# Sooner query loads and unturned inner gradients in a four-layer forward and backward kernel on one Trainium2 core

## The chip, the cores and the metric

The kernel runs on one core of a Trainium2 chip (trn2). The metric is the device time of one execution in microseconds (us). Three timed executions of the kernel before the change took 1105.07, 1106.90 and 1107.01 us; the median is 1106.9 us. One more execution was recorded by the profiler; it took 1113.49 us, and its recorded span is 1111.6 us.

The names used below: PE is the matrix engine (PEld its weight loads), DVE the vector engine, ACT the scalar engine, POOL the GpSimd engine, SP the sync engine, which here only issues DMAs. DMAs are issued from two engines: from SP (all loads, all transposing DMAs, most stores) and from POOL (the stores written as `k.st.dma_start`). Each engine works through its own list in order, so an instruction that waits holds up everything behind it on that engine.

## What is computed

The forward pass has four layers on x of 2048 tokens by 512: linear attention (l=0), a gated unit or GLU (l=1), linear attention with the same weights (l=2), the GLU again (l=3). Each is `x = x + layer(layernorm(x))`.

```python
def A(x):   # 32 heads of 16
    q, k, v = split(x @ wqkv)
    pq, pk = phi(q), phi(k)          # phi(t) = where(t > 0, t + 1, exp(t)) + 1e-6
    kv, z = sum_s(pk * v), sum_s(pk)
    return ((pq @ kv) / (pq . z + 1e-6)) @ wo
def B(x):   # inner width 1376
    return (sigmoid(x @ w_gate) * (x @ w_up)) @ w_down
```

The outputs are the result, and the gradients of x, wqkv, wo, w_gate, w_up and w_down for a given gradient of the result, all in bfloat16.

## The kernel before

**Tiling.** Tokens are cut into 16 tiles of 128 rows, four tiles to a block (`NBLK` = 4 blocks of 512 tokens, `SB` = 512). The inner width 1376 is cut into 11 chunks (`NFC`) of 128; as 1376 is 10 times 128 plus 96, the last chunk starts at 1248 and repeats 32 rows (`FDUP`) of the tenth (`FC0`). A matmul here takes a 128x128 weight block and 512 columns.

**Stages, in order of time.**
1. l=0 forward (`AFwd.first`, `AFwd.second`), to about 74 us, its second half running on into l=1.
2. l=1 forward (`b_fwd`, L671), 74 to 214 us: for each block, 11 chunks of gate and up products (`glu`, L642), then the down product of the block before (`down`, L681). Meanwhile the second half of l=0 is stepped along, one piece per chunk (`next(second)`), in the order of the string `ORDER_0`; its pieces `oBJ` (`out`, L578) finish x for tile J of block B and then ask for the layer norm of that tile (`nxt.need`). The norm of a pair of tiles (`LN.one`, L278) ends in a transposing DMA (L323) from `h_t` to `hT_t`, which the matmuls of the next block read. In block b, chunk 10 asks for the whole block b+1 (L703).
   Each chunk leaves two arrays for the backward pass, kept together as `sd_t`, two chunks to a tile. `store` (L675) writes one chunk at a time to `sv_sd` in DRAM, 256 KB each.
3. l=2 forward, 214 to about 264 us.
4. l=3 forward and backward fused (`b_both`, L719), 264 to 518 us. For each chunk: gate, up, and `dhh` (the gradient coming back through `wdT`, L753); the scaled inner gradient `dd` overwrites `sd_t` (`scale`, L737; the POOL product L662 comes before it). The weight-gradient stage needs `dd` with tokens on partitions, that is turned. For block 0 `dd` is stored unturned to `sv_ddT` (`store_dd`, L814) and turned later by the load. For blocks 1 to 3 it is turned at once by an SBUF-to-SBUF transposing DMA (`turn_dd`, L792) into `nat_t` and stored four chunks at a time to `sv_ddN` (`flush_nat`, L808).
   In block 0 the weights turned for the backward pass are loaded when the last piece of l=2 is done: `load_b_bwd` (L431) issues two transposing loads (L433, L434) into `wuT`, then two into `wgT`, and after each pair a POOL memset (L435) that zeroes the 32 repeated rows of the last chunk, so that they don't count twice. `down(0)` and then `dh_b` (L819) follow in block 1: `dh_b` runs, for each token tile, 11 matmuls with `wuT` and 11 with `wgT` (L825).
5. l=2 backward, first part (`a_bwd1`, L987), 518 to 567 us. For each block b and each of four column chunks dc: four `dq_ps` matmuls, an ACT copy `dq_sb` (`k.mark`, L1035), a DVE product with `qp_l` (L1037), a `t_ps` matmul and three more products in `soft` (L1012). The block ends with 16 `CT_ps` matmuls over `qn_l` (`sums`, L1006). The loads are `qp_l` and `dqT_t` (`loads`, L995: L1001, L1002, 512 KB each) and `qn_l` (L1030, 512 KB). `loads(b+1)` is called at dc=1 of block b and held by a semaphore until that `dq_sb` copy; `qn_l` of block b is loaded at the head of block b. `Fill` (L227) puts matmuls of the l=3 down-weight gradient (`fill_ps`) between them; its own input `hf_t` comes by a transposing load (L240).
6. l=2 backward, second part (`a_bwd2`), l=1 backward (`b_bwd`, L899, which loads `sv_sd` 1 MB at a time, L928), l=0 backward with `a_bwd1` again (759 to 803 us) and `a_bwd2`.
7. Weight gradients, from 862.7 us to the end (`dw_cols` L1232, `dw_rows`, `dw_small`). Each `set_t` piece (`pieces`, L1215) is one block of 512 tokens by up to 512 columns: either a transposing load (L1222) or, for blocks 1 to 3 of l=3, a plain load of `sv_ddN` (L1220). `p_set` has 12 buffers there (6 for the first group).

**What sets the order.** The Tile framework orders the instructions of each engine with a planner: it goes by program order, but takes what its own estimate of times says is ready. So the order on SP is not the order of the lines; `held(k, first, load)` adds a semaphore wait on `first` to a load, and `after` adds an order.

The functions that the diff touches and what calls them:

Of the kernel before, what the change touches and what calls it, by code (L numbers as in the profile page):

```python
# [7 lines left out]
BF16 = mybir.dt.bfloat16  # L8
# [9 lines left out]
F = 1376  # L18
# [52 lines left out]
def kernel(  # L71
# [42 lines left out]
    for l in range(4):  # L114
        d = dict(h=dram.tile([S, D], BF16, name=f"sv_h{l}"))
        if l % 2 == 0:
            for nm in ("dqT", "dkT"):
                d[nm] = dram.tile([D, S], BF16, name=f"sv_{nm}{l}")
            for nm in ("hT", "pkT", "qr", "qn"):
                d[nm] = dram.tile([NBLK, P, (2 if nm == "qr" else 1) * NB * D], BF16, name=f"sv_{nm}{l}")  # L120
            d["E"] = dram.tile([D, D], BF16, name=f"sv_E{l}")
            d["M"] = dram.tile([D, D], BF16, name=f"sv_M{l}")
            d["kvT"] = dram.tile([NDC * P, P], BF16, name=f"sv_kvT{l}")
            d["CT"] = dram.tile([D, D], BF16, name=f"sv_CT{l}")
            d["dkvT"] = dram.tile([NDC * P, P], BF16, name=f"sv_dkvT{l}")
        else:
            d["hhT"] = dram.tile([F, S], BF16, name=f"sv_hhT{l}")
            d["ddT"] = dram.tile([2, F, S], BF16, name=f"sv_ddT{l}")
            if l == 3:
                d["g"] = k.g_in  # L130
                d["wd"] = dram.tile([F, D], F32, name="sv_wd3")
                d["ddN"] = dram.tile([NBLK, len(SETS), P, 2, NB, D], BF16, name="sv_ddN3")
            else:
                d["g"] = dram.tile([S, D], BF16, name=f"sv_g{l}")
                d["sd"] = dram.tile([NBLK, NFC, P, 2 * SB], BF16, name=f"sv_sd{l}")
        k.sv.append(d)
    k.rstd = [k.keep.tile([P, NST], F32, name=f"rstd{l}") for l in range(4)]
    k.A = {l: {} for l in (0, 2)}
    k.wT = [dram.tile([P, NDC * D], BF16, name=f"wT{i}") for i in range(6)]
    k.wdT_d = dram.tile([P, NDC * F], BF16, name="wdT_d")  # L140
    k.turned = []
# [85 lines left out]
class Fill:  # L227
# [15 lines left out]
    def run(self):  # L243
        k, nc = self.k, self.k.nc
        ahead = self.load(0)
        for fc in range(NFC):
            t, w = ahead
            ps = k.bank([P, D], F32, name="fill_ps")
            for st in range(NST):
                if st == 3 and fc + 1 < NFC:  # L250
                    ahead = self.load(fc + 1)
                nc.tensor.matmul(ps[0:w, :], lhsT=t[:, st, 0:w], rhs=self.g[st // NB][:, st % NB, :],  # L252
                                 start=(st == 0), stop=(st == NST - 1))
# [172 lines left out]
def turn_wd(k, t, i):  # L426
    c0, w = SETS[i]
    k.nc.sync.dma_start_transpose(out=t[:, :, c0:c0 + w], in_=k.w_in["wd"][c0:c0 + w, :])


def load_b_bwd(k, t, nm, first):  # L431
    nc = k.nc
    held(k, first, nc.sync.dma_start_transpose(out=t[:, 0:NFC - 1, :], in_=k.w_in[nm][:, 0:(NFC - 1) * P]))  # L433
    nc.sync.dma_start_transpose(out=t[:, NFC - 1, :], in_=k.w_in[nm][:, F - P:F])  # L434
    nc.gpsimd.memset(t[0:FDUP, NFC - 1, :], 0.0)  # L435

# [10 lines left out]
class AFwd:  # L447
# [130 lines left out]
    def out(self, b, j):  # L578
        k, nxt = self.k, self.nxt
        y_ps = k.bank([P, D], F32, name="y_ps")  # L580
        mm4(k, y_ps[:], lambda c: self.pe[b, c // 2][:, 0, c % 2, rows(j)], lambda c: self.M[:, c, :])
        add_x(k, b * NB + j, y_ps, None if self.l else narrow(k, b * NB + j))
        if j % 2 and (b < 2 or self.l == 0) and not (b and j == NB - 1 and self.l == 0):
            nxt.need(b * NB + j)

    def second(self, nxt):
# [34 lines left out]
        if l == 2:  # L621
            k.wdT = k.p_wa.tile([P, NDC, F], BF16, name="wdT", tag="wkvo")
            turn_wd(k, k.wdT, 0)
            last_grads(k, 0)
# [46 lines left out]
def b_fwd(k, l, ln, nxt):  # L671
# [3 lines left out]
    def store():  # L675

        b, fc, hh, sd = late.pop()
        store_hh(k, sv, b, fc, hh, nc.sync)
        nc.sync.dma_start(out=sv["sd"][b, fc], in_=sd.rearrange("p a b -> p (a b)"))

# [10 lines left out]
    for b in range(NBLK):  # L691
# [3 lines left out]
        for fc in range(NFC):  # L695
            hh, sd = glu(k, ln.hT[b], fc, fc % 2 == 1, b == fc == 0)
            hhs[b].append(hh)
            if late:
                store()
            late.append((b, fc, hh, sd))  # L700
            if fc == NFC - 1:
# [17 lines left out]
def b_both(k, l, ln, ctx):  # L719
# [17 lines left out]
    def scale(b, fc, dhh, dd):  # L737
        k.last_mul = nc.vector.tensor_tensor(dd, dhh[:].unsqueeze(1).to_broadcast([P, 2, SB]), dd, ALU.mult)  # L738
        if b:
            turn_dd(k, sv, b, fc, dd)  # L740
        else:
            store_dd(k, sv, b, fc, dd, nc.sync)

    late = []
    for b in range(NBLK):
# [4 lines left out]
        for fc in range(NFC):  # L750
            hh, dd = glu(k, ln.hT[b], fc, first=b == fc == 0)
            ps = k.bank([P, SB], F32, name="dhh_ps")
            mm4(k, ps[:], lambda c: k.wdT[:, c, FC0[fc]:FC0[fc] + P], lambda c: gTs[b][:, c, :])  # L753
            dhh = k.p_dhh.tile([P, SB], BF16, name="dhh_t")
# [37 lines left out]
def turn_dd(k, sv, b, fc, dd):  # L792
# [8 lines left out]
    if f == 1:  # L801
        flush_nat(k)
    if f == 3 or fc == NFC - 1:
        w = SETS[i][1]
        k.nats.append((sv["ddN"][b, i, :, :, :, 0:w], k.nat[:, :, :, 0:w]))
# [27 lines left out]
def backward(k):  # L833
    nc, tc = k.nc, k.tc
    with ExitStack() as ctx:
# [10 lines left out]
        sv, k.n_t, k.turn = k.sv, NB, True  # L846
        k.wdT = w_pool(k, "wdT").tile([P, NDC, F], BF16, name="wdT")
        k.fill = Fill(k)
# [50 lines left out]
def b_bwd(k, l):  # L899
    nc, sv = k.nc, k.sv[l]  # L900
    with ExitStack() as ctx:
# [23 lines left out]
        for b in range(NBLK):  # L925
            for f0, nf in FGRP:
                sh = k.p_sh.tile([P, 4, 2, SB], BF16, name="sh_t", tag="sh")
                nc.sync.dma_start(out=sh[:, 0:nf].rearrange("p f a s -> p f (a s)"),  # L928
                                  in_=sv["sd"][b, f0:f0 + nf].rearrange("f p s -> p f s"))
                for fc in range(f0, f0 + nf):  # L930
                    i = fc - f0
                    ps = k.bank([P, SB], F32, name="dhh_ps")
                    mm4(k, ps[:], lambda c: k.wdT[:, c, FC0[fc]:FC0[fc] + P], lambda c: gTs[b][:, :, c, :])
                    dhh = p_g.tile([P, SB], BF16, name="dhh_t")
# [52 lines left out]
def a_bwd1(k, l, big, ph1, p_dq):  # L987
# [4 lines left out]
    CT_ps = [k.bank2([P, D], F32, name="CT_ps") for _ in range(NDC)]  # L992
    late, gs, dqTs, qps = [], k.early, [], []

    def loads(b):  # L995

        if b % 2 == 0:
# [4 lines left out]
               nc.sync.dma_start(out=flat(dqTs[b]), in_=sv["qr"][b][:, half:2 * half]))  # L1002
        if b:
            held(k, k.mark, *lds)

# [16 lines left out]

    loads(0)
    gs.append(a_grads(k, 2))
    k.fill.step(12)
    for b in range(NBLK):
        g_t, gT = gs[b]
        qp, dqT = qps[b // 2][:, b % 2], dqTs[b]
        qn = big.tile([P, NDC, NB, P], BF16, name="qn_l", tag=f"big{b % 2}")
        nc.sync.dma_start(out=flat(qn), in_=sv["qn"][b])  # L1030
        for dc in range(NDC):
# [12 lines left out]
            if dc == 1 and b + 1 < NBLK:  # L1044
                loads(b + 1)
                if b == 1 and l == 2:
# [168 lines left out]
def pieces(k, nat, src, c0, w, turned=None):  # L1215

    for b in range(NBLK):
        t = k.p_set.tile([P, NB, w], BF16, name="set_t", tag="set_t")
        if turned is not None and b:
            k.nc.sync.dma_start(out=t[:], in_=turned[b, c0 // D, :, :, 0:w])  # L1220
# [79 lines left out]
```

## Time and profile before

| what | value |
|---|---|
| timed executions | 1105.07, 1106.90, 1107.01 us, median 1106.9 us |
| profiled execution, its own time | 1113.49 us |
| its span | 1111.6 us |
| busy: PE | 1063.4 us (96%) |
| busy: DVE, ACT, POOL | 554.7, 445.6, 302.3 us |
| share of 16 DMA engines' span, SP's queue | 75.5% |
| share of 16 DMA engines' span, POOL's queue | 13.3% |

A line of the timeline or of the chain of waits starts with the time in us since the start of the span and a length in us. "SPq" is SP issuing a DMA; the length is how long the issue occupied SP, not the transfer. In the table of waits, a line reads: engine, line of the kernel, what waited, what ended the wait; then total us, number of times, longest. In the table of stretches, the columns after the stretch are its length, the busy us of each engine with the number of instructions in brackets, the clock that PE was granted (1.00 is full), the share of DMA engine time in use, and GB/s.

### The profile page before, as it was taken

Reading aid. Unit: us, or ns where it says so; the run is one execution under the profiler, and the core shown is the slowest. Engines: PE = TensorE matmul, PEld = TensorE weight load, DVE = VectorE, ACT = ScalarE, POOL = GpSimd, SP = SyncE. Lnnn points to the kernel's source line nnn. Section 1 sums busy time; section 2 is a strip of 40 time slices with the busy share of each in tenths; the row PEclk is TensorE's granted clock in tenths of the full one; section 3 lists DMA queues with packets and bytes.
Section 4 is the critical chain, followed back from the end, with each engine's and each line's share of the span. In section 5 each row is a group of like instructions: output and inputs, shape, how many; then the busy total and the mean of one; then the engine's idle time right before and its main releaser. Section 6 shows DMA issues by size and latency. Waiting matters only on the chain.

```text
span 1111.6 us, 15216 instructions
## 1 busy us (share of the span) xinstructions
PE 1063.4 (96%) x5355; PEld 496.4 (45%) x5448; DVE 554.7 (50%) x1029; ACT 445.6 (40%) x930; POOL 302.3 (27%) x404
## 2 busy tenths in 40 slices
PE   6989899998979999999899999999999999999998
PEld 3444343444434444444344444444444444465443
DVE  7696764669825544444668445555876200001110
ACT  3476766547743737363224434433235200000010
POOL 5333433203622616140542210001623100011110
PEclk9999999999989999999999999999999999999999
DMA  8998987689995979899997997879989899599990
GB/s 246 254 269 246 274 218 223 197 199 206 268 249 132 264 192 245 224 236 267 329 279 237 235 261 228 230 180 246 356 252 335 227 257 212 124 199 254 250 222 34
DMA packets 394973, 259.99 MB, mean 234 GB/s; under 512 B 305745, under 2 KB 356721, under 8 KB 393873
## 3 DMA queue, kind: packets, MB, share of 16 engines
q1 hardware_dynamic: 379648, 208.91, 75.5%
q0 software_dynamic: 15248, 50.11, 13.3%
q8 instruction: 42, 0.69, 0.3%
q14 instruction: 35, 0.28, 0.1%
HBM read 77.73 MB, written 106.76 MB: 166 GB/s over the span
## 4 chain that ended last, share of the span: by engine, by line
PE 55%; DMA 3%; ACT 1%; issue 1%; DVE 1%; POOL 1%; SPq 0%; ACTq 0%; DVEq 0%; POOLq 0%
PE dw_ps L1244 18%; PE dh_ps L916 6%; PE dh_ps L1089 4%; PE dhh_ps L196 4%; PE dh_ps L825 3%; PE dw_ps L1262 3%; PE dh_ps L1080 2%; PE dpk_ps L196 2%; PE CT_ps L1009 2%; PE y_ps L196 2%; PE fill_ps L252 2%; PE dq_ps L196 1%; PE g_ps L196 1%; PE u_ps L196 1%; DMA qp_l<-sv_qr 1%
## 5 line engine op out<-in xcount | busy, mean ns | idle before, releaser
L1244 PE MATMUL dw_ps<-set_t,rows_t 128*128 128x512 bf16 (+1 forms) x1008 | 203.6, 362 | 0.8
L1244 PEld LDWEIGHTS <-rows_t 128*128 128x128 bf16 x1024 | 100.2, 98 | 103.6
L662 POOL TENSOR_TENSOR sd_t<-sd_t,hh_t 128x512 bf16<-128x512 bf16 x68 | 81.4, 1197 | 157.0 <-DVE hh_t L657 104.7
L1169 DVE CAST dw_new<-dw_ps 128x512 bf16<-128x512 f32 (+1 forms) x20 | 12.4, 654 | 186.9 <-PE dw_ps L1244 186.5
L1169 ACT CAST dw_new<-dw_ps 128x512 bf16<-128x512 f32 (+1 forms) x20 | 10.5, 561 | 225.7 <-PE dw_ps L1244 188.1
L886 ACT ACTIVATE t_sb<-dh_ps,rstd 128x512 f32<-128x512 f32 x64 | 43.5, 680 | 130.8 <-PE dh_ps L825 81.1
L196 PE MATMUL g_ps<-hT_t,wg 128*128 128x512 bf16 (+1 forms) x360 | 91.6, 377 | 4.0 <-DMA hT_t<-h_t 2.5
L196 PE MATMUL u_ps<-hT_t,wu 128*128 128x512 bf16 (+1 forms) x360 | 91.3, 377 | 0.5 <-DVE hh_t L657 0.2
L196 PE MATMUL dhh_ps<-gT_t,wdT 128*128 128x512 bf16 x342 | 89.0, 379 | 1.3 <-ACT dhh_t L935 1.0
L916 PE MATMUL dh_ps<-wgT,dd_t 128*128 128x512 bf16 x174 | 66.0, 379 | 0.4
L657 DVE SCALAR_TENSOR_TENSOR hh_t<-sd_t,u_ps 128x512 bf16<-128x512 bf16 x88 | 59.5, 679 | 10.1 <-ACT sd_t L656 9.4
L916 PE MATMUL dh_ps<-wuT,dd_t 128*128 128x512 bf16 x169 | 64.1, 379 | 0.1
L738 DVE TENSOR_TENSOR sd_t<-dhh_t,sd_t 128x1024 bf16<-128x1024 bf16 x44 | 30.4, 690 | 65.4 <-POOL sd_t L662 63.9
L1170 POOL DMA_DIRECT2D out_dram<-dw_new x36 | 19.2, 541 | 156.1 <-DVE dw_new L1169 136.0
L656 ACT ACTIVATE sd_t<-g_ps,onef 128x512 bf16<-128x512 f32 x88 | 60.4, 690 | 2.6
L937 DVE TENSOR_TENSOR dd_t<-dhh_t,sh_t 128x1024 bf16<-128x1024 bf16 x44 | 30.0, 690 | 59.0 <-ACT dhh_t L935 52.9
L655 ACT ACTIVATE g_ps<-g_ps 128x512 f32<-128x512 f32 x88 | 52.6, 601 | 11.5 <-PE g_ps L196 11.5
L196 PEld LDWEIGHTS <-wg 128*128 128x128 bf16 x360 | 34.6, 98 | 45.2 <-issue 3.5
L196 PEld LDWEIGHTS <-wu 128*128 128x128 bf16 x360 | 35.4, 98 | 42.1 <-issue 1.8
L196 PEld LDWEIGHTS <-wdT 128*128 128x128 bf16 x352 | 34.4, 98 | 42.6 <-issue 1.6
L825 PEld LDWEIGHTS <-sd_t 128*128 128x128 bf16 x352 | 34.5, 98 | 41.5
L916 PEld LDWEIGHTS <-dd_t 128*128 128x128 bf16 x352 | 34.4, 98 | 41.5
(167 smaller groups left out, 1839.1 us busy)
## 6 DMA issues: line engine op xcount, KB each, us to landing
sv_sd<-sd_t SPq DMA_DIRECT2D x44, 256.0 KB, 3.2
sv_ddT<-dd_t SPq DMA_DIRECT2D x40, 256.0 KB, 5.0
sv_h<-h_t POOLq DMA_DIRECT2D x16, 512.0 KB, 5.4
sv_qr<-pe_t POOLq DMA_DIRECT2D x16, 512.0 KB, 5.2
sh_t<-sv_sd SPq DMA_DIRECT2D x8, 1024.0 KB, 6.9
rows_t<-sv_h SPq DMA_DIRECT2D x16, 512.0 KB, 7.7
sv_ddN<-nat_t SPq DMA_DIRECT2D x6, 1024.0 KB, 5.1
set_t<-sv_ddN SPq DMA_DIRECT2D x12, 512.0 KB, 6.4
```

The source lines that it names most:

```text
L196: i = k.nc.tensor.matmul(out, lhsT=lhs(c), rhs=rhs(c), start=(c == 0), stop=(c == n - 1))
L655: nc.scalar.activation(g_ps[:], g_ps[:], ACT.Tanh, scale=-0.5)
L656: nc.scalar.activation(sd[:, 0, :], g_ps[:], ACT.Identity, bias=k.onef[:], scale=-1.0)
L657: nc.vector.scalar_tensor_tensor(hh[:], sd[:, 0, :], 0.5, u_ps[:], ALU.mult, ALU.mult)
L662: nc.gpsimd.tensor_tensor(sd[:, 1, :], sd[:, 1, :], hh[:], ALU.mult)
L738: k.last_mul = nc.vector.tensor_tensor(dd, dhh[:].unsqueeze(1).to_broadcast([P, 2, SB]), dd, ALU.mult)
L825: k.nc.tensor.matmul(dh_ps[:], lhsT=dds[fc][:, a, rows(j)], rhs=(k.wuT, k.wgT)[a][:, fc, :], start=(i == 0), stop=(i == 2 * NFC - 1))
L886: nc.scalar.activation(t_sb[:], dh_ps, ACT.Identity, scale=rstd, accum_out=c1[:])
L916: nc.tensor.matmul(acc[b][j][:], lhsT=dd[:, a, rows(j)], rhs=(k.wuT, k.wgT)[a][:, fc, :], start=(fc == 0 and a == 0), stop=(fc == NFC - 1 ...
L1089: nc.tensor.matmul(dh[j][:], lhsT=lhs(j, c), rhs=rhs(c), start=False, stop=stop and c == NDC - 1)
L1244: k.nc.tensor.matmul(ps[ic][:, 0:w], lhsT=h_m[:, ic * P:(ic + 1) * P], rhs=t_m, start=(m == 0), stop=(m == n - 1))
L1262: k.nc.tensor.matmul(p[0:r, :], lhsT=t[:, f:f + r], rhs=g_t, start=(i == 0 and st == 0), stop=(i == len(srcs) - 1 and st == NST - 1))
```

## The change

There are seven edits.

1. **Last chunk padded with zeros.** `wdT` is widened to 11 times 128 columns; the 32 columns ahead of the last 96 are zeroed by a POOL memset, and the last part is loaded by two transposing DMAs in place of one. `dhh` and so `dd` are then zero in the repeated rows, and the two memsets of `wuT` and `wgT` go.
2. **Norm of l=1 asked for sooner.** The last pair of tiles of blocks 2 and 3 is asked for by `out`, at the end of its own block of l=0, and no longer at chunk 10.
3. **`sv_sd` two chunks at a time.** The layout becomes partition first; a store covers two chunks (512 KB), the loads of `b_bwd` read one run per partition.
4. **Order of the last two chunks in `turn_dd`.** For blocks 1 and 2, chunk 10 is turned before chunk 9, which then overwrites the zero columns.
5. **Block 3 of l=3** is stored unturned (`store_dd`), and the tail turns it by a transposing load.
6. **`qn_l` sooner.** `qn_l` of block b+1 is loaded at dc=1 of block b, held by that copy; that of block 0 before the loop.
7. **`qp_l` and `dqT_t` sooner.** Those of block 1 are loaded after the first 12 fill matmuls, held by the last of them; those of block b+2 at dc=1 of block b.

```diff
-                d["sd"] = dram.tile([NBLK, NFC, P, 2 * SB], BF16, name=f"sv_sd{l}")
+                d["sd"] = dram.tile([P, NBLK * NFC, 2 * SB], BF16, name=f"sv_sd{l}")
...
-                nc.tensor.matmul(ps[0:w, :], lhsT=t[:, st, 0:w], rhs=self.g[st // NB][:, st % NB, :],
+                self.last = nc.tensor.matmul(ps[0:w, :], lhsT=t[:, st, 0:w], rhs=self.g[st // NB][:, st % NB, :],
...
 def turn_wd(k, t, i):
     c0, w = SETS[i]
+    n = (NFC - 1) * P
+    if i == len(SETS) - 1:
+        k.nc.gpsimd.memset(t[:, :, n:n + FDUP], 0.0)
+        k.nc.sync.dma_start_transpose(out=t[:, :, n + FDUP:], in_=k.w_in["wd"][n:F, :])
+        w = n - c0
     k.nc.sync.dma_start_transpose(out=t[:, :, c0:c0 + w], in_=k.w_in["wd"][c0:c0 + w, :])
...
     nc.sync.dma_start_transpose(out=t[:, NFC - 1, :], in_=k.w_in[nm][:, F - P:F])
-    nc.gpsimd.memset(t[0:FDUP, NFC - 1, :], 0.0)
...
-        if j % 2 and (b < 2 or self.l == 0) and not (b and j == NB - 1 and self.l == 0):
+        if j % 2 and (b < 2 or self.l == 0) and not (b == 1 and j == NB - 1 and self.l == 0):
             nxt.need(b * NB + j)
...
         store_hh(k, sv, b, fc, hh, nc.sync)
-        nc.sync.dma_start(out=sv["sd"][b, fc], in_=sd.rearrange("p a b -> p (a b)"))
+        n = b * NFC + fc
+        if n % 2:
+            nc.sync.dma_start(out=sv["sd"][:, n - 1:n + 1], in_=sd[:].rearrange("p n a s -> p n (a s)"))
...
-        if b:
+        if 0 < b < NBLK - 1:
+            if fc == NFC - 2:
+                return
             turn_dd(k, sv, b, fc, dd)
+            if fc == NFC - 1:
+                turn_dd(k, sv, b, fc - 1, dds[b][fc - 1])
         else:
             store_dd(k, sv, b, fc, dd, nc.sync)
...
-                                  in_=sv["sd"][b, f0:f0 + nf].rearrange("f p s -> p f s"))
+                                  in_=sv["sd"][:, b * NFC + f0:b * NFC + f0 + nf])
...
-        if b:
-            held(k, k.mark, *lds)
+        return lds
+
+    def rows_n(b):
+        qns[b] = big.tile([P, NDC, NB, P], BF16, name="qn_l", tag=f"big{b % 2}")
+        return nc.sync.dma_start(out=flat(qns[b]), in_=sv["qn"][b])
...
     loads(0)
+    rows_n(0)
     gs.append(a_grads(k, 2))
     k.fill.step(12)
+    held(k, k.fill.last, *loads(1))
     for b in range(NBLK):
         g_t, gT = gs[b]
         qp, dqT = qps[b // 2][:, b % 2], dqTs[b]
-        qn = big.tile([P, NDC, NB, P], BF16, name="qn_l", tag=f"big{b % 2}")
-        nc.sync.dma_start(out=flat(qn), in_=sv["qn"][b])
+        qn = qns[b]
...
             if dc == 1 and b + 1 < NBLK:
-                loads(b + 1)
+                held(k, k.mark, rows_n(b + 1), *(loads(b + 2) if b + 2 < NBLK else ()))
...
-        if turned is not None and b:
+        if turned is not None and 0 < b < NBLK - 1:
             k.nc.sync.dma_start(out=t[:], in_=turned[b, c0 // D, :, :, 0:w])
         else:
             k.nc.sync.dma_start_transpose(out=t[:], in_=src[c0:c0 + w, b * SB:(b + 1) * SB])
```

More of the change, by code (lines that the diff above doesn't have):

```diff
@@ L139 @@
     k.wT = [dram.tile([P, NDC * D], BF16, name=f"wT{i}") for i in range(6)]
-    k.wdT_d = dram.tile([P, NDC * F], BF16, name="wdT_d")
+    k.wdT_d = dram.tile([P, NDC * NFC * P], BF16, name="wdT_d")
     k.turned = []
@@ L621, in second @@
         if l == 2:
-            k.wdT = k.p_wa.tile([P, NDC, F], BF16, name="wdT", tag="wkvo")
+            k.wdT = k.p_wa.tile([P, NDC, NFC * P], BF16, name="wdT", tag="wkvo")
             turn_wd(k, k.wdT, 0)
@@ L699, in b_fwd @@
                 store()
-            late.append((b, fc, hh, sd))
+            late.append((b, fc, hh, k.sd2))
             if fc == NFC - 1:
@@ L752, in b_both @@
             ps = k.bank([P, SB], F32, name="dhh_ps")
-            mm4(k, ps[:], lambda c: k.wdT[:, c, FC0[fc]:FC0[fc] + P], lambda c: gTs[b][:, c, :])
+            mm4(k, ps[:], lambda c: k.wdT[:, c, rows(fc)], lambda c: gTs[b][:, c, :])
             dhh = k.p_dhh.tile([P, SB], BF16, name="dhh_t")
@@ L802, in turn_dd @@
         flush_nat(k)
-    if f == 3 or fc == NFC - 1:
+    if f == 3 or fc == NFC - 2:
         w = SETS[i][1]
@@ L846, in backward @@
         sv, k.n_t, k.turn = k.sv, NB, True
-        k.wdT = w_pool(k, "wdT").tile([P, NDC, F], BF16, name="wdT")
+        k.wdT = w_pool(k, "wdT").tile([P, NDC, NFC * P], BF16, name="wdT")
         k.fill = Fill(k)
@@ L932, in b_bwd @@
                     ps = k.bank([P, SB], F32, name="dhh_ps")
-                    mm4(k, ps[:], lambda c: k.wdT[:, c, FC0[fc]:FC0[fc] + P], lambda c: gTs[b][:, :, c, :])
+                    mm4(k, ps[:], lambda c: k.wdT[:, c, rows(fc)], lambda c: gTs[b][:, :, c, :])
                     dhh = p_g.tile([P, SB], BF16, name="dhh_t")
@@ L992, in a_bwd1 @@
     CT_ps = [k.bank2([P, D], F32, name="CT_ps") for _ in range(NDC)]
-    late, gs, dqTs, qps = [], k.early, [], []
+    late, gs, dqTs, qps, qns = [], k.early, [], [], {}
     def loads(b):
```

## The prediction

> **What bounds the kernel now.** I read the page first: PE is busy for 96% of the span and the chain that ended last is mostly matmuls, so time can only come from the 4% in which PE stands still, and from stretches in which it runs at a lower clock.
>
> ```profile
> PE 1063.4 (96%) x5355; PEld 496.4 (45%) x5448; DVE 554.7 (50%) x1029; ACT 445.6 (40%) x930; POOL 302.3 (27%) x404
> PE 55%; DMA 3%; ACT 1%; issue 1%; DVE 1%; POOL 1%; SPq 0%; ACTq 0%; DVEq 0%; POOLq 0%
> ```
>
> Next the table of waits for PE, which says where that 4% lies (1111.6 - 1063.4 = 48.2 us in all, much of it in pieces too small to be listed). Start-up (5.9) is untouched by the change; four of the other large ones are in its reach:
>
> ```profile
> PE y_ps L196 <- DVE hh_t L657: 5.8, 1, 5.8
> PE dq_ps L196 <- ACT dq_sb L1035: 4.5, 7, 1.8
> PE g_ps L196 <- DMA hT_t<-h_t: 2.5, 1, 2.5
> PE CT_ps L1009 <- DMA qn_l<-sv_qn: 2.3, 1, 2.3
> PE fill_ps L252 <- DMA hf_t<-sv_hhT: 2.0, 1, 2.0
> ```
>
> The timeline around the longest shows its true cause. POOL waits from 313.7 until `wuT` has landed, to do a 0.5 us memset; behind it stand the products of `sd_t`, behind those DVE, and behind DVE the PSUM banks that PE wants:
>
> ```profile
> 318.41 5.86 SPq L433 DMA_TRANSPOSE wuT<-in_B_w_up_dram  x1
> 325.63 5.32 SPq L433 DMA_TRANSPOSE wgT<-in_B_w_gate_dram  x1
> 327.85 0.51 POOL L435 MEMSET wuT<- 32x512 bf16 x1 [14.11 <-DMA wuT<-in_B_w_up_dram]
> 330.86 4.09 PE L196 MATMUL y_ps<-wd,hh_t 128*128 128x512 bf16 x11 [5.78 <-DVE hh_t L657]
> ```
>
> The chain of waits names the loads of `a_bwd1`:
>
> ```profile
> 528.43 4.62 DMA qp_l<-sv_qr
> 537.04 7.45 DMA qp_l<-sv_qr
> 557.00 4.52 DMA qn_l<-sv_qn
> 759.89 7.72 DMA hf_t<-sv_hhT
> ```
>
> Last, sums over stretches, which show the clock and the two passes of `a_bwd1`:
>
> ```profile
> 177.00:180.40 3.40, 1.29 (x6) 0.39 (x4) 2.53 (x8) 0.20 (x1) 0.00 (x0) 1.00 1.09 224
> 180.40:183.80 3.40, 3.00 (x8) 1.05 (x9) 0.00 (x0) 1.08 (x2) 0.00 (x0) 0.50 0.16 61
> 764.10:767.50 3.40, 1.53 (x7) 0.50 (x6) 3.40 (x8) 2.37 (x5) 0.00 (x0) 1.00 1.04 316
> 520.30:566.90 46.60, 40.13 (x173) 17.49 (x175) 29.76 (x59) 15.99 (x29) 19.79 (x19) 0.96 1.04 300
> 761.90:802.80 40.90, 38.34 (x175) 17.27 (x176) 33.41 (x68) 14.34 (x26) 20.41 (x20) 1.00 1.06 326
> ```
>
> A stretch of 3.4 us with PE busy for 1.29 is followed by one at clock 0.50; one with 1.53 (764.1) is not. The stretches at 323.8 (1.28), 327.2 (0.00) and 559.3 (1.13) are followed by 0.50 too. So a gap above some 2 us costs itself and about half of the next 3.4 us. The page "TensorE: Matmul & The Clock Gate" of the Trainium skill (Why this matters for your kernels) asks only that gaps stay under some 3 us; by it the gaps of 2.5 and 2.3 would cost nothing beyond themselves, and the sum below would be 3.2 us smaller. The rows speak against it here.
>
> **The change part by part.** A matmul takes 0.216 us (four in 0.86).
>
> *Norm sooner (edit 2).* At 180.80 PE waits 2.51 us for the last transposed pair of block 2. Its load is issued at 174.97, after the norm of chunk 10; now it is asked for after `y_ps` of tile 11, near 160, so it lands some 8 us ahead of 178.3. Then the 8 matmuls from 180.80 to 184.02 ran in 3.22 us and would take 1.73. Gain 2.51 + 1.49 = 4.0 us. Next late is DVE freeing banks; at the same border one block earlier (127.35) that was 0.55, so at least 3.4. The moved work (ACT two squares of 0.9 and a 0.2, DVE two of 0.55, POOL 0.9, one transposing DMA of 1.3 to 1.9 on SP) falls in 160 to 168, where ACT is busy for 12 of 20 us; if that cover failed, it would cost the 2 us of ACT.
>
> *Memsets gone (edit 1).* Without the POOL wait PE runs `down(0)` through: 317.79 + 44 x 0.216 = 327.3, then 11 matmuls with `wuT` to 329.7. Now `wgT` is late. Today the second memset starts at 334.46, released by `wgT`, so it is there at 334.4 and no sooner, since SP is still issuing it until 332.2. The first `wgT` matmul started at 337.15; it could start at 334.4, 2.75 us sooner. But a gap of 4.7 us is left, with a slow clock after it (1.6 us, by half of 3.17 as after 330.86), and freed POOL and DVE now issue two 128 KB and two 256 KB stores beside the loads, 0.77 MB, up to 3.5 us at the 227 GB/s of 320 to 325. Ends: gain 2.75, loss 2.75 - 1.6 - 3.5 = 2.35. The nearest row is the gap of 5.78 itself, replaced by one of about its size: I take 0. The new memset is on 128x128 elements (the old 32x512 took 0.51) and waits for nothing; the extra transposing DMA costs SP about 1.25 (row of L434), somewhere in 253 to 278 while SP has a wait of 3.7 at 277.7 for `qn_t`; uncovered, it delays `wuT` by 1.25, inside these ends.
>
> *`a_bwd1`, first pass (edits 6, 7).* The passes do the same matmuls. The second takes 40.9 us, of which 1.98 is the `hf_t` gap: 38.9. The first takes 46.6. The difference, 7.7, agrees with its gaps: 0.36 + 1.71 (535.00) + 1.78 (546.45) + 2.31 (561.57) + 1.7 of slow clock from 562.7 = 7.9. `qp_l` of block 1 now leaves SP behind two transposing DMAs of `ga_t` in place of three; the one of block 2 a whole block earlier; `qn_l` of block 3 goes ahead of the `hf_t` load that holds SP from 547.32 to 556.96. But the DMA engines are already at 1.04, and 2 MB of `woT` and `wqkvT` stay in the middle, so not all comes back. Ends: 7.7, and 4.0 if only the `qn_l` gap goes (2.31 + 1.7). The middle of the three changed loads, 4 to 8 us earlier against a wait of under 2, is the nearest: I take 6.5.
>
> *`a_bwd1`, second pass.* The 1.98 gap at 767.66 is `hf_t`, issued at 759.89. `qn_l` of block 0 used to follow it at 763.92; now it may go first: 512 KB at 326 GB/s is 1.6 us more of gap. Or SP, which has fewer loads behind, lets `hf_t` go sooner and the gap closes. Ends: loss 4 (1.6 more, and a slow clock), gain 2. I take a loss of 1.0.
>
> *Block 3 unturned (edits 4, 5).* Eleven transposing DMAs of 1.3 to 3 us and three stores leave SP and POOL between 470 and 506, eleven plain stores come; PE has no gap from 440 to 520, so 0. In the tail six plain loads (0.37 us on SP) become transposing ones (1.36, as at 949.05). Four of these in a row took 9.50 us of SP from 884.54, about 2.4 each; a piece is 16 matmuls, 3.45 us of PE, and SP waits there 54.9 + 15.2 us for free buffers. So 0; with that cover gone, 6 x (2.4 - 0.4) = 12. The page "Advanced Engine Details and Errata" (X-Bar Transpose) has such DMAs as fast as plain ones; by it even the uncovered price would be nothing. The rows (2.4 against 0.5 for the three plain loads from 894.09) say otherwise.
>
> *`sv_sd` in pairs (edit 3).* 22 fewer issues of about 0.5 on SP, the same bytes; PE waits for none of them. The pair frees its tile about 2 us later (512 KB stores land in 5.4, 256 KB in 3.2), with seven tiles in rotation. Ends +0.5 and -1; I take 0.
>
> **Sum.** 4.0 + 0 + 6.5 - 1.0 = 9.5 us. The profiled execution took 1113.49 (span 1111.6); so 1104.0. The timed runs' median is 1106.9, a factor of 0.994, so 1097.5.
>
> **Rivals.**
> - *Everything pays:* 4.0 + 2.75 + 7.7 + 2.0 = 16.4, that is 1091. For it: the second pass shows that the pace is possible. Against: `wgT` is late by the row.
> - *Sooner, but the transfers are the bound:* 3.4 - 2.0 + 4.0 - 1.6 = 3.8, that is 1103. For it: DMA share 1.04 and 1.06 in both passes. Against: the wanted bytes, 1.5 MB a block in 9.7 us, are half of the 300 GB/s moved.
> - *The planner leaves the queue as it was,* so that the query loads leave no sooner: only the 4.0 of the norm, 1103. For it: SP's order is not program order even now (two `qn_l` at 517.91).
> - *Slower: the sooner loads overtake the fill's transposing loads on SP.* In the first pass `qn_l` of block 0 waits for memory until 517.89 and `dqT_t` until 521.08; if the planner sets both ahead of `hf_t` (now issued at 510.05, wanted at 523.8; `hf_t` takes 5.8 to 12.3 us to land between 500 and 580, I take 8.3), it lands at 529.4: 5.6 of gap and 1.6 of clock. In the second, three loads ahead of it are 1.5 MB, 4.6 us, and 1.6 of clock. Then 4.0 + (6.5 - 7.2) - 6.2 = -2.9, that is 1109.8. It decides once the first `hf_t` leaves after 515.5. Against: the planner puts off what it thinks not ready.
>
> **How the numbers follow.** Forecast 0.50; everything pays 0.08; transfers bound 0.22; order unchanged 0.12; slower 0.08. The forecast's own ends (memsets from -2.35 to 2.75, first pass 4.0 to 7.7) give some 1094 to 1102. To leave out no more than 2 in 10 the range goes from 1091 to 1105. A measurement tells about 0.2% (2.2 us) from no change. Faster by more (below 1104.7): 0.50 + 0.08 + 0.17 + 0.10 = 0.85; within: 0.09; slower: 0.06.
>
> **What would show it.** Right: no PE wait on `hT_t` near 178; POOL without a wait on `wuT`, and PE waiting about 4 to 6 us for `wgT` between the `wuT` and `wgT` halves of L825; no DVE wait on `qp_l`, no PE wait on `qn_l`, a first pass of 39 to 41 us; PE waiting 2 to 4 us for `hf_t` in the second; no idle before L1244. Wrong: a gap on `set_t` in the tail, a first pass above 43, or `wgT` early enough that the gap at L825 is under 2.

## The result and the profile after

Four timed executions of the changed kernel took 1108.49 to 1110.82 us, median 1109.62, beside 1106.62 for the kernel before. The ratio is 1.003, with a 95% interval of 1.0013 to 1.0047: the change costs about 3 us, where 9.4 us of gain were predicted. Three of the timed executions of the kernel before in the experiments, of 1118 to 1123 us, are over 1.5% above the fastest of their set and are left out of the comparisons. The profiled execution of the changed kernel took 1110.82 us; its span is 1109.1.

The page of after, busy time of PE and the chain that ended last:

```profile
PE 1068.2 (96%) x5448; PEld 495.4 (45%) x5448; DVE 553.2 (50%) x1029; ACT 445.1 (40%) x930; POOL 301.4 (27%) x403
PE 56%; DMA 2%; ACT 2%; DVE 1%; issue 1%; POOL 1%; ACTq 0%; POOLq 0%; DVEq 0%
```

(Before's 1063.4 lacks some matmul records, 5355 against 5448, so the two busy times can't be set against each other.) The table of PE's waits after (us in total, times, longest):

```profile
PE dh_ps L835 <- DMA wgT<-in_B_w_gate_dram: 4.4, 1, 4.4
PE fill_ps L252 <- DVE dkT_t L1115: 3.6, 1, 3.6
PE y_ps L692 <- DVE hh_t L661: 3.0, 2, 2.2
PE fill_ps L252 <- DMA hf_t<-sv_hhT: 2.4, 1, 2.4
PE CT_ps L1022 <- DMA qn_l<-sv_qn: 0.5, 1, 0.5
```

The waits on `hh_t` (5.8), on `dq_sb` (4.5, now 1.1), on `hT_t` (2.5) and on `qn_l` (2.3, now 0.5) are gone or small, as the prediction said; the 3.0 on `hh_t` at L692 stands for 2.0 at L686 in before. Two of their size are new. One was foreseen: `wgT`, which the timeline shows at the place where the POOL wait was:

```profile
312.93 7.60 SPq L438 DMA_TRANSPOSE wuT<-in_B_w_up_dram  x1
321.89 6.76 SPq L438 DMA_TRANSPOSE wgT<-in_B_w_gate_dram  x1
...
324.96 2.54 PE L835 MATMUL dh_ps<-wuT,sd_t 128*128 128x512 bf16 x11
331.94 4.85 PE L835 MATMUL dh_ps<-wgT,sd_t 128*128 128x512 bf16 x11 [4.45 <-DMA wgT<-in_B_w_gate_dram]
```

The other, 3.59 us at 585.60, lies in `a_bwd2`, a stage that the prediction did not look at. Stretches of after: the border at 177, the first pass of `a_bwd1`, `a_bwd2` (from the first `dkvT_ps` matmul to the first `dhh_ps` of `b_bwd`), and the second pass:

```profile
177.00:180.40 3.40, 3.40 (x18) 1.51 (x17) 0.92 (x3) 0.00 (x0) 0.00 (x0) 1.00 1.06 410
517.48:556.98 39.50, 38.80 (x178) 17.19 (x176) 29.50 (x59) 16.21 (x30) 19.80 (x19) 1.00 1.05 303
556.98:629.08 72.10, 68.20 (x329) 31.21 (x328) 42.75 (x78) 27.68 (x69) 19.85 (x21) 0.98 0.83 249
757.98:800.49 42.51, 38.98 (x177) 17.33 (x176) 32.26 (x68) 14.52 (x26) 20.56 (x20) 1.00 1.06 318
```

The same three stages of before:

```profile
520.30:567.13 46.83, 40.36 (x174) 17.59 (x176) 29.76 (x59) 16.22 (x30) 19.79 (x19) 0.96 1.04 300
567.13:633.80 66.67, 65.99 (x322) 30.84 (x328) 43.75 (x78) 27.67 (x69) 19.96 (x21) 1.00 0.89 241
761.90:802.98 41.08, 38.52 (x175) 17.34 (x176) 33.41 (x68) 14.52 (x26) 20.41 (x20) 1.00 1.06 327
```

The first column after the stretch is its length. The first pass is 7.33 us shorter; `a_bwd2`, which the diff does not touch, is 5.43 longer, and the second pass 1.43 longer. How `a_bwd2` loses them is seen by following the gap at 585.60 back, in the timeline of after (SP, then DVE, then PE):

```profile
562.40 10.17 SPq L240 DMA_TRANSPOSE hf_t<-sv_hhT  x1
572.67 0.52 SPq L1083 DMA_DIRECT2D haT_l<-sv_hT  x1
573.29 0.38 SPq L1085 DMA_DIRECT2D pkT_l<-sv_pkT  x1
...
580.24 0.69 DVE L1108 TENSOR_SCALAR dph_t<-pkT_l 128x2048 bf16<-128x2048 bf16 x1 [4.25 <-DMA pkT_l<-sv_pkT]
...
585.60 3.25 PE L252 MATMUL fill_ps<-gf_t,hf_t 128*128 128x512 bf16 x8 [3.59 <-DVE dkT_t L1115]
```

and at the same step of before:

```profile
572.56 4.76 SPq L240 DMA_TRANSPOSE hf_t<-sv_hhT  x1
578.38 0.34 SPq L1069 DMA_DIRECT2D haT_l<-sv_hT  x1
581.84 0.33 SPq L1071 DMA_DIRECT2D pkT_l<-sv_pkT  x1
...
586.60 0.69 DVE L1094 TENSOR_SCALAR dph_t<-pkT_l 128x2048 bf16<-128x2048 bf16 x1 [0.45 <-DMA pkT_l<-sv_pkT]
```

In both kernels this `hf_t` is issued 5.4 us after the first `dkvT_ps` matmul (562.40 - 556.98 and 572.56 - 567.13). In before SP is held for 4.76 us by it, in after for 10.17: eight loads of 512 KB stand in front of it, the last of which landed at 573.58 in before and at 572.85 in after. PE has come 10.15 us sooner, the last of the loads only 0.7 (the first of the eight was issued 4.6 us sooner, at 552.39 in place of 557.00; why the eight then took longer to land is not shown). So `haT_l` and `pkT_l` of block 2, behind `hf_t` on SP, are late for a PE that is early; DVE waits 4.25 us for `pkT_l` in place of 0.45, and behind that instruction stand the layer norm's products and the emptying of the PSUM banks, for which PE waits 3.59 us and then runs at half clock for one 3.41 us window.

### The profile page after: what moved, and what is told of

Its sections match the earlier page's. It is cut to its first block, busy times and chain, and to the rows that moved or that the text cites. A ratio compares the mean times of both kernels' runs of the same rounds, so it can differ in the third digit from the quotient of the medians.

```text
span 1109.1 us, 15241 instructions
## 1 busy us (share of the span) xinstructions
PE 1068.2 (96%) x5448; PEld 495.4 (45%) x5448; DVE 553.2 (50%) x1029; ACT 445.1 (40%) x930; POOL 301.4 (27%) x403
## 4 chain that ended last, share of the span: by engine, by line
PE 56%; DMA 2%; ACT 2%; DVE 1%; issue 1%; POOL 1%; ACTq 0%; POOLq 0%; DVEq 0%
PE dw_ps L1258 18%; PE dh_ps L926 7%; PE dh_ps L1103 4%; PE dhh_ps L196 4%; PE dh_ps L835 3%; PE dw_ps L1276 3%; PE dh_ps L1094 3%; PE CT_ps L1022 2%; PE fill_ps L252 2%; PE dpk_ps L196 2%; PE dq_ps L196 2%; PE y_ps L196 2%; PE g_ps L196 1%; PE u_ps L196 1%; DMA hf_t<-sv_hhT 1%
## 5 line engine op out<-in xcount | busy, mean ns | idle before, releaser
L926 PE MATMUL dh_ps<-wuT,dd_t 128*128 128x512 bf16 x176 | 66.7, 379 | 0.0
L926 PE MATMUL dh_ps<-wgT,dd_t 128*128 128x512 bf16 x176 | 66.7, 379 | 0.0
L252 PE MATMUL fill_ps<-gf_t,hf_t 128*128 128x512 bf16 (+1 forms) x176 | 49.3, 388 | 6.0 <-DVE dkT_t L1115 3.6
L196 PEld LDWEIGHTS <-wu 128*128 128x128 bf16 x360 | 35.2, 98 | 41.5 <-issue 0.7
```

The source lines that it names most:

```text
L196: i = k.nc.tensor.matmul(out, lhsT=lhs(c), rhs=rhs(c), start=(c == 0), stop=(c == n - 1))
L252: self.last = nc.tensor.matmul(ps[0:w, :], lhsT=t[:, st, 0:w], rhs=self.g[st // NB][:, st % NB, :], start=(st == 0), stop=(st == NST - 1))
L926: nc.tensor.matmul(acc[b][j][:], lhsT=dd[:, a, rows(j)], rhs=(k.wuT, k.wgT)[a][:, fc, :], start=(fc == 0 and a == 0), stop=(fc == NFC - 1 ...
```

## The experiments

Each was timed against the kernel before on the same chip. Over the sets the kernel before had medians of 1107.3 to 1108.7, and single executions from 1100.8 to 1115.1, so a median tells about 2 to 3 us, and the stages of the profiled executions have to say where. All profiled executions, in us ("l=1" is from the second block of the l=1 GLU to the first `E_ps` matmul of l=2, "l=3" from its first block to its second, "1st" and "2nd" the passes of `a_bwd1`; lengths are between the first matmuls of each stage):

| kernel | l=1 | l=3 | 1st | `a_bwd2` | 1st + `a_bwd2` | 2nd | median | ratio to before, 95% |
|---|---|---|---|---|---|---|---|---|
| before | 107.4 | 89.0 | 46.8 | 66.7 | 113.5 | 41.1 | 1106.6 | |
| after | 106.7 | 88.5 | 39.5 | 72.1 | 111.6 | 42.5 | 1109.6 | 1.003 (1.0013 to 1.0047) |
| e1 before again | 107.7 | 88.4 | 45.3 | 66.7 | 112.0 | 41.1 | 1106.8 | 0.9978 (0.9951 to 1.0005) |
| e2 after again | 106.7 | 96.6 | 39.8 | 71.5 | 111.4 | 44.2 | 1112.7 | 1.0019 (0.9995 to 1.0044) |
| e3 only the loads | 107.3 | 88.3 | 47.2 | 68.6 | 115.8 | 43.6 | 1111.3 | 1.0017 (0.9991 to 1.0043) |
| e4 all but the loads | 106.7 | 86.5 | 45.4 | 66.7 | 112.1 | 40.8 | 1110.4 | 1.0005 (0.9979 to 1.0032) |
| e5 `hf_t` behind | 106.7 | 86.8 | 47.2 | 66.7 | 113.8 | 42.0 | 1107.6 | 1.001 (0.9985 to 1.0035) |
| e6 halves | 106.7 | 81.6 | 42.6 | 69.1 | 111.8 | 43.9 | 1106.0 | 1.0003 (0.9972 to 1.0034) |
| e7 block 3 turned | 104.9 | 86.8 | 40.3 | 72.8 | 113.1 | 41.5 | 1111.9 | 1.0035 (1.0011 to 1.0059) |
| e8 three mends | 106.6 | 81.6 | 39.7 | 67.0 | 106.8 | 41.1 | 1099.1 | 0.9919 (0.9888 to 0.995) |
| e9 mends, no loads | 105.0 | 81.6 | 50.6 | 66.7 | 117.2 | 40.7 | 1104.4 | 0.9962 (0.9944 to 0.998) |
| e10 `qn_l` first too | 105.0 | 91.2 | 40.7 | 66.7 | 107.4 | 41.1 | 1100.4 | 0.9939 (0.9912 to 0.9965) |
| e11 two orders only | 106.7 | 86.1 | 44.4 | 66.7 | 111.1 | 42.5 | 1106.1 | 0.999 (0.9964 to 1.0015) |
| e12 before, mended | 107.1 | 93.2 | 42.8 | 66.7 | 109.5 | 41.0 | 1106.5 | 1.0007 (0.9976 to 1.0038) |

The theory: the sooner loads do gain in the first pass, and the gain is handed back in `a_bwd2` and the second pass, by the order on SP. The rivals: the profiled execution of before was an unlucky one and there was nothing to gain; the transfers set the pace, whatever the order; the clock and the transfers of a single execution make the differences.

**e1 and e2: both kernels once more.** No edit.

> The kernel before, unchanged, profiled once more and timed against itself. Theory A (hand-back: the sooner loads do gain some 7 us in the first pass of a_bwd1, and a_bwd2, whose own loads come no sooner, gives 5 back): the first pass takes 46 to 47 us again and the profiled span is near 1111. Theory B (the profiled execution of before was not like the timed ones; its first pass was slower by the luck of DMA times): the first pass takes 39 to 42 us here and the span is near 1105. Timed ratio 1.000 within 0.002 by both.

> The kernel after, unchanged, profiled and timed once more. Both theories: about 1109.6 us, ratio 1.002 to 1.004. Its profile should again have a first pass of 39 to 40 us, the wait of fill_ps in a_bwd2 of 3 to 4 us behind DVE and pkT_l, and 4 to 5 us of waiting for wgT; if the wait in a_bwd2 is absent here, it was luck.

The stages came back: 45.3 and 66.7 in before, 39.8 and 71.5 in after. Part of before's length was of that one execution (1113.49, with a first pass of 46.8, is above all its first timed runs), but the exchange between the two stages was not. The 45.3 lies between what the two theories had for e1, nearer to theory A; the wait of `fill_ps` behind `dkT_t` in e2 was 2.9, a little under its range. In time the loss is there again: e2's median is 5.9 us above e1's, of the same set, and its ratio of 1.0019 has an interval that just reaches 1 (0.9995).

**e3 and e4: the change taken in two.** e3 is the kernel before with edits 6 and 7 alone, e4 the kernel after without them. The heart of both edits:

```diff
-                loads(b + 1)
+                held(k, k.mark, rows_n(b + 1), *(loads(b + 2) if b + 2 < NBLK else ()))
```

> The kernel before with edits 6 and 7 alone (query loads and qn_l sooner). Theory A: gain 7, hand-back 5, second pass -1: 1105 to 1107, ratio 0.998 to 1.000. Theory B: no gain in the timed runs and the hand-back and the later hf_t stay as losses: 1108 to 1112, ratio 1.002 to 1.005.

> The kernel after without edits 6 and 7. Theory A: the other edits are the loss: 1108 to 1112, ratio 1.002 to 1.005. Theory B: the other edits gain the 1 to 2 us that the norm and the memsets show in the profile: 1104 to 1106, ratio 0.998 to 1.000.

Without the loads (e4), `a_bwd2` and the second pass are those of before to 0.3 us: the losses there belong to edits 6 and 7. With the loads alone (e3) `a_bwd2` and the second pass lose, 1.95 and 2.4, and yet the first pass took 47.2: `qn_l` was late by 1.00 and 3.93 there. That fell outside what the theory had. The times settle nothing: neither ratio (1.0017 and 1.0005) is clear of 1, and that of e4 lies between its two theories. For the first pass of e3 two causes were open, block 3's transposing DMAs (e7) and the loads' own order (e10, e11).

**e5: `hf_t` behind `pkT_l`.**

```diff
+        if fc == 4:
+            after(self.k, ld, self.k.pk_ld)
```

`ld` is the `hf_t` load of the fifth chunk of the fill, `pk_ld` the `pkT_l` load issued last in program order, that of block 2.

> The kernel after, with one load moved: the transposing load of hf_t for the fifth chunk of the fill is issued on SP behind the pkT_l load of block 2 of a_bwd2 instead of ahead of it. Theory A (what the first pass gained is handed back because pkT_l of block 2 is late behind that hf_t, which held SP for 10.2 us): the gap of 3.59 us before fill_ps (released by dkT_t on DVE) and the slow clock behind it go; from the first dkvT matmul to the first dhh matmul of b_bwd 66.7 to 68 us in place of 72.1; the timed median 4 to 5 us below that of the kernel after. Theory B (DMA bandwidth, not the order on SP, makes pkT_l late: seven loads of 512 KB are in flight): pkT_l lands late all the same, the stage stays above 70 us and the median is within 2 us of the kernel after.

`a_bwd2` took 66.67. But this execution had a late first pass as well, by a new gap of 4.86 us for `qn_l`, so its `a_bwd2` had no early PE to keep up with, and the run alone does not tell the theories apart. (e3's `a_bwd2`, without this order and behind an equally late first pass, took 68.6.) The 4 to 5 us of theory A did not show in the time: the median is 2 us below the 1109.6 of after, which is of another set, and the ratio is 1.001. The timeline of e5 shows why `qn_l` of block 2 was late:

```profile
530.49 6.66 SPq L238 DMA_TRANSPOSE hf_t<-sv_hhT  x1
537.25 0.53 SPq L1017 DMA_DIRECT2D qn_l<-sv_qn  x1
```

After had the same two at 529.88 (5.62) and 535.60, and its `qn_l` landed at 540.06 without a wait; here it landed at 543.89. In e3 the late `qn_l` was the same one, behind the same `hf_t` (issued at 538.68, landed at 545.68). The first pass of the changed kernel stands at an edge, and some executions fall off it.

**e6: halves.** In `dh_b` of block 0 all four tiles go through the `wuT` matmuls before any goes through those of `wgT`.

```diff
-        for i in range(2 * NFC):
-            a, fc = divmod(i, NFC)
+    for a in range(2):
+        for j in range(NB):
+            for fc in range(NFC):
```

> The kernel after, with dh_b of block 0 done by halves: the wuT matmuls of all four tiles (44, 9.5 us) before the wgT matmuls of any. Theory A (the wait for wgT that took the memset's place is on the path): the gap of 4.45 us at the wgT matmuls and the slow clock behind it go, the stretch from the first chunk of block 0 to that of block 1 of the second GLU goes from 88.5 to 82.5 to 84.5 us, and the timed median falls by 4 to 6 us. Rival: the four tiles then come to ACT and DVE together, 2.4 us apart in place of 4.75, the PSUM banks are freed late, and 2 to 4 us of it come back as gaps released by ACT or DVE: stretch of 85 to 88 us, median within 3 us of the kernel after.

The stretch went to 81.58, a little under what was expected, and no gap for a bank came in its place. The median, 1106.0, is 3.7 us below after's, which is of another set; by the ratios (1.0003 and 1.003) it is 2 to 3 us, and the intervals overlap, so the time does not decide between theory A (4 to 6) and the rival (within 3). Of the profiled executions, e6's span is 5.8 us below after's (1103.3 and 1109.1), where the place gained 6.9; the waits for `dkT_t` (2.3) and `hf_t` (2.3) were there in after too, that of 2.6 for `qn_l` was not.

**e7: block 3 turned at once, the rest of the change kept.**

```diff
-        if 0 < b < NBLK - 1:
+        if b:
             if fc == NFC - 2:
```

> The kernel after without its unturned block 3: the inner gradients of block 3 are turned at once by eleven transposing DMAs, as in the kernel before, and loaded plainly in the tail; the sooner loads stay. Theory A1 (the sooner loads come in time only because block 3's eleven transposing DMAs have left SP): first pass of a_bwd1 of 44 to 47 us as in the kernel with the loads alone (47.2), in place of 39.5, time 5 us above the kernel after. Theory A2 (the sooner loads gain by themselves, and the 47.2 was the clock and DMA times of one execution): first pass of 39 to 42 us, time within 2 us of the kernel after.

First pass 40.3, `a_bwd2` 72.8: the loads come in time without edit 5. A2 holds for the stage, and e3's 47.2 was, by its late `qn_l`, the same edge as e5's. The median, 1111.9, is 2.3 above after's of another set, the ratio 1.0035 against 1.003.

**e8: three mends together.** e5's, e6's, and in the second pass the `hf_t` load ahead of `dqT_t` and `qn_l` of block 0.

```diff
+    k.fill.step(0 if l else 12)
+    for ld in (loads(0)[1], rows_n(0)):
+        l or after(k, ld, k.fill.ld)
     gs.append(a_grads(k, 2))
-    k.fill.step(12)
+    k.fill.step(12 if l else 0)
```

> The kernel after with the two edits of the runs before it in this set (hf_t behind pkT_l; wuT half of all four tiles first) and a third: in the second pass the hf_t load is issued ahead of the first dqT_t and qn_l. Theory A (three hand-backs hide the gain): 5 + 5 + 1.5 us less than the kernel after, a median of 1097 to 1101, and no PE gap above 2 us between 310 and 620; gap for hf_t near 765 under 2 us. Theory B (the times are set by where the slow clock windows fall, and each removed gap lets another appear): 1104 or more.

1099.1 us in six executions, 0.9919 of before (0.9888 to 0.995), the fastest of all kernels here and the only one of its set below before by more than the interval. Its profiled span is 13.7 us below after's (1095.4 and 1109.1), and the three places of the mends hold 13.1 of it: 6.9 in l=3, 4.8 in the first pass with `a_bwd2`, 1.4 in the second pass. Neither e5's edit nor e6's by itself was told from before in the time; the third was not run by itself. The timeline of e8, SP and then DVE, shows the mended order:

```profile
561.46 0.33 SPq L1082 DMA_DIRECT2D haT_l<-sv_hT  x1
564.91 0.33 SPq L1084 DMA_DIRECT2D pkT_l<-sv_pkT  x1
565.29 4.29 SPq L238 DMA_TRANSPOSE hf_t<-sv_hhT  x1
...
569.84 0.93 DVE L1107 TENSOR_SCALAR dph_t<-pkT_l 128x2048 bf16<-128x2048 bf16 x1 [0.61 <-DMA pkT_l<-sv_pkT]
```

and its stretches (first pass, `a_bwd2`) show both stages short at once:

```profile
510.47:550.21 39.74, 38.51 (x174) 17.18 (x176) 28.91 (x59) 16.21 (x30) 19.82 (x19) 1.00 1.04 299
550.21:617.23 67.02, 66.15 (x323) 30.84 (x328) 43.01 (x78) 27.68 (x69) 19.11 (x21) 1.00 0.94 269
```

The sum is 106.8, against 111.4 to 115.8 in the nine executions above it in the table; e10, which has the order of e5 too, came to 107.4. The bytes are the same, and 269 GB/s were moved in `a_bwd2` in place of 249: it was the order on SP, not what the DMA engines can carry.

**e9: the mends without the sooner loads.** `a_bwd1` is that of before.

> The kernel with the three mends of the run before (hf_t behind pkT_l, wuT half of all four tiles first, hf_t ahead of qn_l in the second pass), but with the query loads of the kernel before (the parts qn_l sooner and qp_l, dqT_t sooner undone). Theory A (the sooner query loads gain in the first pass, and only the hand-backs hid it): first pass of 45 to 47 us, a_bwd2 stage of 66.7, a median 4 to 7 us above the 1099.1 of the kernel with the mends and the loads, thus 1103 to 1106. Theory B (the mends alone made the gain; the loads are worth nothing in the time): 1098 to 1101.

1104.4 us, as theory A had it; its first pass was longer than expected (50.6, with 4.12 for `dq_sb` and 2.63 for `qn_l`). With the hand-backs mended, the sooner loads are worth 1104.4 - 1099.1 = 5.3 us of the median (the two come from different sets; by the ratios 0.4 points, with intervals that just overlap). e10, of e9's own set and with the loads and one more order, was 3.9 us below e9.

**e10: and `qn_l` of block 2 ahead of its `hf_t`.**

```diff
-                held(k, k.mark, rows_n(b + 1), *(loads(b + 2) if b + 2 < NBLK else ()))
+                held(k, k.mark, rows_n(b + 1))
+                if l and b == 1:
+                    k.fill.ahead = k.fill.load(2)
+                held(k, k.mark, *(loads(b + 2) if b + 2 < NBLK else ()))
```

> The kernel with the three mends and a fourth: in the first pass of a_bwd1 the qn_l load of block 2 leaves SP ahead of the transposing hf_t load that held SP for 5.6 to 6.7 us in front of it. Theory A (the first pass took 39.5 in some executions and 47.2 in others because this qn_l lands within 1 us of being wanted, behind hf_t): first pass of 39 to 40.5 us, no gap released by qn_l in it, median 1095 to 1098 with a spread of under 5 us over the runs. Theory B (the first pass varies by the speed of the transfers, whatever the order): a spread of 7 us or more and a median within 1.5 us of 1099; or hf_t is now late in its turn, with a gap released by hf_t near 535.

Theory A fell, and the signs of theory B came: 1100.4 with executions from 1096.7 to 1108.1, and `hf_t` late in its turn by 1.06. This profiled execution also waited for `wuT`, so that even e6's mend did not cover it:

```profile
331.69 11.52 PE L836 MATMUL dh_ps<-wuT,sd_t 128*128 128x512 bf16 x43 [7.10 <-DMA wuT<-in_B_w_up_dram]
```

**e11: after with the two orders of the first pass alone** (e5's and e10's edits).

> The kernel after with nothing but two orders on SP changed, both in the first pass and behind it: qn_l of block 2 ahead of its hf_t, and pkT_l of block 2 of a_bwd2 ahead of its hf_t. The wait for wgT and the second pass are those of the kernel after. Theory A (first pass plus a_bwd2 came to 111 to 114 us in the kernel before and in seven of the eight others, because what comes sooner in the one waits in the other, and these two orders are the whole cause): first pass 39 to 40.5 and a_bwd2 stage 66.5 to 67.5, together 106 to 108; wgT gap of 3.5 to 4.5 us as in after; median 1103 to 1106. Theory B (it needs the other mends too, since the phase of the clock and the transfers decide): together 111 or more, median 1107 or more.

`a_bwd2` 66.67 as expected, but a first pass of 44.4, with PE waiting for the `hf_t` that was put back:

```profile
542.25 1.03 PE L252 MATMUL fill_ps<-gf_t,hf_t 128*128 128x512 bf16 x2 [3.28 <-DMA hf_t<-sv_hhT]
```

The sum of the two stages, 111.1, is what theory B had; the median, 1106.1, lies between the two, and the wait for `wgT` was 2.6 rather than 3.5 to 4.5. So moving `qn_l` past `hf_t` only trades one wait for the other; the mend that holds is that of `pkT_l`.

**e12: the kernel before with the mends that fit it.**

> The kernel before, with nothing of the change, and with the mends that can be put on it: pkT_l of block 2 ahead of hf_t, the wuT half of all four tiles of dh_b first, the fill's load asked for ahead of the second pass's first loads. Theory A (the gain is of the change, and the mends only keep it from being handed back): the gap of some 5.8 us that the memsets make near 330 stays, first pass 45 to 47, a_bwd2 66.7, and the median is within 2 us of the kernel before. Theory B (the mends gain by themselves, whatever the change): the stretch from block 0 to block 1 of the second GLU falls to 82 to 85 us and the median is 3 us or more below the kernel before.

1106.5, ratio 1.0007 (0.9976 to 1.0038): the mends alone are worth nothing that can be told. PE's wait for `hh_t` behind the memset was 8.1 here, where it was 5.8 in before and 3.9 in e1 and e3. Without the sooner loads the first pass ranged from 42.8 to 50.6 over five executions.

## Why the prediction was wrong

Means over the profiled executions that had an edit and those that had not, beside the terms as predicted (e10 and e11, which have e10's order in the first pass, are left out from the row of `a_bwd1` on):

| term | predicted | measured | executions |
|---|---|---|---|
| norm sooner (l=1) | -4.0 | 106.1 - 107.4 = -1.2 | 10, 4 |
| memsets gone (l=3, without e6's halves) | 0 | 88.5 - 88.6 = 0.0 | 6, 3 |
| `a_bwd1`, first pass | -6.5 | 42.3 - 46.2 = -3.9 | 7, 5 |
| `a_bwd2` (without e5's order) | not named | 70.8 - 66.7 = +4.2 | 5, 5 |
| `b_bwd` | not named | 128.7 - 128.2 = +0.5 | 7, 5 |
| second pass (without e8's order) | +1.0 | 43.0 - 41.0 = +1.9 | 6, 3 |
| weight-gradient tail | 0 | 249.1 - 249.1 = 0 | 2, 2 |
| sum | -9.5 | +1.5 | |

The sum of +1.5 lies at the lower end of the timed +1.4 to +5.2 (0.0013 and 0.0047 of 1106.6). The rest, 1.8 us to the middle of that interval, is not given a place; the l=3 stretch, from 86.1 to 96.6 where edit 1 is in, is the least steady one and could hold them, but that was not shown. Single executions differ by several us in these stages, so the table says where the time went and not to a tenth: the two means of the first pass come from 39.5 to 47.2 and from 42.8 to 50.6, and the 0.5 in `b_bwd`, for which no cause was shown, may be chance.

- **The step that failed** is "`a_bwd1`, first pass ... I take 6.5". The place was read rightly, but the size was not: the 39.5 of after lay within the 39 to 41 foretold, and the mean is 42.3, a gain of 3.9. In three of the seven executions `qn_l` of block 2, which still stands behind a transposing `hf_t` load, came 2.6 to 4.9 us late. And the sum put nothing down for the stage behind: it did not ask what is late next once PE leaves the pass 7 us sooner. Behind it the next loads stand on SP behind one transposing load, and they did not move with PE; `a_bwd2` took 4.2 us more in the mean, as much as the pass had gained. The signs that were to tell right from wrong all lay inside the changed places, so they came out "right" (but for 0.5 us for `qn_l` in the second pass) in a kernel that was slower.
- **Norm sooner**: the wait at 178 is gone as said, but the term was mis-sized. It gave 1.2 in place of 4.0. A gap of 0.8 for `hh_t` came at 172 in its place, and the 1.49 for the clock was hardly the edit's: each of the four executions without it had one half-clock window in this stage, two (before and e3) at 180 and two near 136, at a gap that both kernels have (below); of the ten with it, seven had one near 136 and three had none.
- **Memsets gone** came out at 0 in the mean, by the mechanism foretold: `wgT` late by 4.45 in after, a slow clock behind it. The 0 hangs on e2's 96.6, where PE also waited 4.40 for `hT_t`; without it the mean is 86.9, a gain of 1.6, and the sum of the table would be about 0.
- **Second pass**: the sign was right; `hf_t` was issued at 756.45, behind `dqT_t` and `qn_l`, held SP for 5.22 and landed at 765.27. The loss is 1.9 rather than 1.0.
- **Block 3 unturned and `sv_sd` in pairs**: no gap in the tail, 249.1 in both kernels. Right.
- **The slower rival** gave 1109.8 and the time was 1109.6, but its mechanism took place only in the second pass; that the numbers agree is luck. In the first pass `hf_t` was not overtaken; it was `hf_t` that held `qn_l` and `pkT_l`. **Transfers as the bound** is refuted by e8 (the same bytes, 4.8 us less in the two stages), though its terms for the two passes, 4.0 of gain and 1.6 of loss, came nearer to the means than the forecast's.
- The terms were taken from an execution of 1113.49, higher than 107 of the 123 timed executions of before; the factor of 0.994 mends the level, not the sizes of the gaps. The rule that a gap above some 2 us costs half of the next 3.4 us leaves out where the gap lies; that comes out below.

## What to carry to other kernels

When a load is moved sooner and PE with it, follow SP's queue on into the next stage and ask of each load there whether it moves too; look first for a transposing load with plain loads in front of it and something wanted soon behind it. A gain is proven by the sum of the changed stage and the next ones, not by the gap that went, and by several executions when one window of clock is worth 1.7 us. A change that looks worthless may need only the order of what stands behind it: here two orders of loads and one of matmuls, together, made 3 us of loss into 9 us of gain.

## What the runs showed of the hardware

**A transposing load can hold its queue until the loads in front have all but landed.** The issue of `hf_t` on SP ended at 552.34 and 572.57 in after, where the last plain load in front landed at 552.57 and 572.85; in e5 537.15 and 555.08 against 537.28 and 555.35; in e10 538.02 and 555.22 against 538.33 and 555.45. In the 14 profiled executions 62 issues of `hf_t` held SP for over 5 us, and 60 of them ended within 0.9 us of the moment when the last of the plain transfers issued by SP in front had landed. It is no rule without exception: in the second pass one issue of each execution (in after at 769.79, 3.10 us) ended 2 to 4 us ahead of that landing, and what it is that frees the issue was not shown. In before at 572.56, where the last load in front landed 1.0 us later, it took 4.76. So its price on SP depends on what is in front of it, and a plain load that is moved ahead of it can hold up everything behind it.

**The clock goes by a grid.** The slow windows of every execution lie on a grid of 3.413 us, which begins anywhere. In 14 profiled executions, past the start-up, a window of that grid at full clock was followed by one at half clock in every case in which PE was busy for less than 41% of it (35 windows), and in none from 44% up (between them both occurred). So a gap of 2.0 to 2.2 us can cost a slow window (some 1.7 us, half of 3.41) if it lies within one window, and no more than itself if a border cuts it, as in before. Stretches on the grid, around the `y_ps` gap near 135, of before (gap 134.63 to 136.62):

```profile
132.64:136.05 3.41, 1.94 (x9) 0.69 (x7) 0.94 (x3) 3.38 (x9) 2.03 (x3) 1.00 1.14 208
136.05:139.47 3.42, 2.85 (x14) 1.32 (x15) 2.16 (x4) 0.65 (x2) 1.95 (x2) 1.00 1.02 363
```

and of after (133.04 to 135.22):

```profile
131.98:135.40 3.42, 1.24 (x6) 0.41 (x5) 2.65 (x4) 2.97 (x6) 2.34 (x3) 1.00 1.14 292
135.40:138.81 3.41, 3.41 (x9) 1.22 (x8) 0.96 (x2) 0.00 (x0) 1.44 (x2) 0.50 1.05 286
```

The second column of numbers is PE's busy time, the last but two the clock: 1.94 of 3.41 leaves the next window at 1.00, 1.24 makes it 0.50. The Trainium skill, page "TensorE: Matmul & The Clock Gate" (What's actually happening), has this window, of 3413 ns and free-running, and the runs agree; it calls the clock slow after an idle window, where these rows show that a window with PE busy for 36% of it is enough.
